# Two row tiles that take turns on PSUM banks: the turn signal moved from the SP queue to POOL, and one small product spread over a half tile

## The chip, the cores and the metric

The kernel runs on one core of a Trainium2 chip. The metric is the device time of one execution in microseconds (us), as the median of several runs.

In the views of the profile PE is TensorE's matmul, PEld its weight load, DVE VectorE, ACT ScalarE, POOL GpSimd and SP SyncE; a q behind a name stands for the instructions that its sequencer runs itself. A row of the windows view has the length of a stretch, then the busy time of PE, PEld, DVE, ACT and POOL (with the number of instructions), the granted clock, the busy share of the DMA engines and GB/s. All times are in us.

## The reference

A layer norm feeds a linear-attention block and a GEGLU feed-forward block, and both are added to the input. S = 2048 rows, D = 576, F = 4608, 32 heads of 18.

```python
xn = _layernorm(x, axis=-1)
return x + _A_ref(xn, A_wqkv, A_wo) + _B_ref(xn, B_w_gate, B_w_up, B_w_down)

# _B_ref: (gelu(x @ w_gate) * (x @ w_up)) @ w_down
# _A_ref: phi(q) @ (phi(k)^T v) / den, per head, then @ wo
```

## The kernel before

After the attention part (about 78 us) the kernel works through four groups of 512 rows. Each group has a gate/up stage of 18 blocks and a down stage of eight half tiles (128 rows by 288 columns of the output, each the sum of 36 down matmuls and five with `m_sb`). The sums stand in PSUM, in eight banks. A block has two units; a unit makes 128 gate and 128 up columns, on two 64-row tiles of the array that work at the same time. D = 576 is 4.5 x 128, so the halves of the fifth chunk of gate and up share one tile of weights (`wr`).

```python
class _Unit:
    def p1(self):                       # first phase: ten matmuls
        for kt in (4, 0, 1, 2, 3):
            self.mm(0, LO, kt, kt == 4, False)           # gate, upper 64 rows
            last = self.mm(1, HI, kt, kt == 4, False)    # up, lower 64 rows
        self.turn = nc.sync.nop()                        # the turn signal
        tc.add_manual_dep(self.turn.ins, last.ins.name, SYNC, ...)

    def p2(self):                       # second phase: eight matmuls, banks exchanged
        for kt in range(4):
            m = self.mm(1, LO, kt, False, kt == 3)
            if kt == 0:
                tc.add_manual_dep(m.ins, self.turn.ins.name, SYNC, ...)
            self.mm(0, HI, kt, False, kt == 3)
```

In the second phase each row tile writes the bank that the other one wrote before. The signal is an instruction without work: it waits until the last matmul of the first phase is done, and the first matmul of the second phase waits for it. It stands in the queue of SP, which issues all DMAs, behind the weight loads of the same unit:

```python
def gu_pair(sc, k):                     # one block
    ...
    for i in range(GUB):
        ...
        if blk > 0:
            load_gu(blk + NWBUF - 1, i) # two DMA issues on SP, for three blocks later
        u.p1()
        units.append((b, u))
    if sc == 0 and k >= 1:
        load_wd_slice()                 # one more DMA issue
    for i, (b, u) in enumerate(units):
        u.p2()
        ...                             # gelu on ACT, product on DVE

def den_norm(sc, c, q, pieces):         # ten of these in stage one, one after a block
    ...
    for h in range(0, w, P):
        nc.vector.reciprocal(out=d[:, h:h + P], in_=d[:, h:h + P])
    nc.gpsimd.tensor_tensor(out=pqT[:rows, c, cols], in0=pqT[:rows, c, cols], in1=d, op=ALU.mult)
```

The product kv x Wo (`m_stage`: ten matmuls of 288 columns into banks 2 to 7 in turn, each copied to `m_sb` by ACT) is made inside the first half tile of the first down stage, which needs it at its end:

```python
hooks = [{0: lambda: m_stage((0, 1, 2)), 16: lambda: m_stage((3, 4))} if sc == 0 else {}]
```

## Time and profile before

| | before |
|---|---|
| median of the first three runs | 532.59 us (532.07 to 533.6) |
| span of the profiled run | 530.5 us |
| TensorE busy | 99% |
| the four gate/up stages | 70.41, 71.39, 70.65, 70.50 us |
| first half tile, and an ordinary one | 7.35, 5.25 us |

### The profile page before, as it was taken

Reading aid. Unit: us, or ns where it says so; the run is one execution under the profiler, and the core shown is the slowest. Engines: PE = TensorE matmul, PEld = TensorE weight load, DVE = VectorE, ACT = ScalarE, POOL = GpSimd, SP = SyncE. Lnnn points to the kernel's source line nnn. Section 1 sums busy time; section 2 is a strip of 40 time slices with the busy share of each in tenths; the row PEclk is TensorE's granted clock in tenths of the full one; section 3 lists DMA queues with packets and bytes.
Section 4 is the critical chain, followed back from the end, with each engine's and each line's share of the span. In section 5 each row is a group of like instructions: output and inputs, shape, how many; then the busy total and the mean of one; then the engine's idle time right before and its main releaser. Section 6 shows DMA issues by size and latency. Waiting matters only on the chain.

```text
span 530.5 us, 10752 instructions
## 1 busy us (share of the span) xinstructions
PE 522.6 (99%) x4532; PEld 314.3 (59%) x4532; DVE 248.7 (47%) x408; ACT 152.5 (29%) x288; POOL 70.3 (13%) x83
## 2 busy tenths in 40 slices
PE   7999999999999999999999999999999999999997
PEld 5887666444467754444477744444677544445775
DVE  7885666783338613333368233333485143333101
ACT  6887783323330003323200022323100132322000
POOL 4666542110002100000012000000021000000000
PEclk9999999999999999999999999999999999999999
DMA  8910006898510025555400055555100345540000
GB/s 283 248 30 1 1 2 184 261 270 267 143 39 12 23 78 153 148 150 157 135 12 12 12 153 162 146 157 153 49 22 13 94 143 158 155 135 1 12 12 22
DMA packets 98810, 55.85 MB, mean 105 GB/s; under 512 B 5322, under 2 KB 98378, under 8 KB 98762
## 3 DMA queue, kind: packets, MB, share of 16 engines
q1 hardware_dynamic: 98762, 55.17, 36.2%
q8 instruction: 35, 0.57, 0.4%
q14 instruction: 13, 0.11, 0.1%
HBM read 52.79 MB, written 2.36 MB: 104 GB/s over the span
## 4 chain that ended last, share of the span: by engine, by line
PE 95%; SPq 2%; DVE 1%; ACT 1%; issue 0%; DMA 0%
PE ps_all L505 51%; PE ps_all L576 27%; PE ps_all L310 4%; PE ps_all L581 4%; PE ps_all L280 4%; PE ps_all L238 3%; PE ps_all L227 1%; SPq L166 1%; PE ps_all L370 1%; SPq L168 0%; SPq L169 0%; DMA x_sb<-in_A_x_dram 0%; ACT xnT L230 0%; DVE xn L217 0%; PE ps_all L358 0%
## 5 line engine op out<-in xcount | busy, mean ns | idle before, releaser
L505 PE MATMUL ps_all<-xnT,wg 64*128 64x512 bf16 x1152 | 274.1, 377 | 0.0
L505 PE MATMUL ps_all<-xnT,wu 64*128 64x512 bf16 x1152 | 272.6, 377 | 0.9 <-SPq L514 0.3
L549 DVE TENSOR_TENSOR hT<-ps_all,gl 128x512 bf16<-128x512 f32 x144 | 99.6, 692 | 168.9 <-ACT gl L548 168.7
L548 ACT ACTIVATE gl<-ps_all 128x512 f32<-128x512 f32 x144 | 86.0, 597 | 316.7 <-PE ps_all L505 294.9
L505 PEld LDWEIGHTS <-wu 64*128 64x128 bf16 x1152 | 106.9, 94 | 70.9 <-SPq L514 8.7
L505 PEld LDWEIGHTS <-wg 64*128 64x128 bf16 x1152 | 107.0, 94 | 66.7 <-issue 0.3
L576 PE MATMUL ps_all<-wd_sb,hT 128*128 128x288 bf16 x1152 | 146.6, 286 | 0.0
L576 PEld LDWEIGHTS <-hT 128*128 128x128 bf16 x1152 | 112.2, 98 | 31.5 <-issue 1.9
L384 DVE RECIPROCAL den_sb<-den_sb 126x128 f32<-126x128 f32 (+1 forms) x80 | 68.3, 911 | 0.5
L385 POOL TENSOR_TENSOR pqT<-pqT,den_sb 126x512 bf16<-126x512 bf16 (+3 forms) x25 | 24.1, 965 | 301.5 <-DVE den_sb L384 298.2
L584 DVE TENSOR_TENSOR res<-ps_all,x_sb 128x288 bf16<-128x288 f32 x32 | 14.6, 458 | 88.3 <-PE ps_all L581 88.3
L505 PE MATMUL ps_all<-xnT,wr 64*128 64x512 bf16 x288 | 55.9, 377 | 0.0
L581 PE MATMUL ps_all<-m_sb,pqT 126*128 126x288 bf16 (+1 forms) x160 | 24.9, 286 | 0.0
L505 PEld LDWEIGHTS <-wr 64*128 64x128 bf16 x288 | 14.6, 94 | 17.4 <-issue 1.1
L310 PE MATMUL ps_all<-xnT,wqkv_sb 128*126 128x512 bf16 (+1 forms) x100 | 24.4, 380 | 0.0
L265 POOL TENSOR_TENSOR hT<-phi_e,phi_a 128x576 bf16<-128x576 f32 x16 | 22.5, 1404 | 8.9 <-ACT phi_e L264 4.9
L280 PE MATMUL ps_all<-hT,xn 128*128 128x288 bf16 (+3 forms) x192 | 23.6, 266 | 0.0
L238 PE MATMUL ps_all<-wqkv_sb,xnT 128*128 128x288 bf16 x160 | 22.4, 286 | 0.8 <-DVE xnT L230 0.6
L280 PEld LDWEIGHTS <-xn 128*128 128x128 bf16 (+1 forms) x192 | 18.2, 101 | 4.5
L320 POOL TENSOR_TENSOR pqT<-phi_e,phi_a 126x512 bf16<-126x512 f32 (+1 forms) x14 | 17.7, 1268 | 15.5 <-DVE phi_a L318 11.8
L581 PEld LDWEIGHTS <-pqT 126*128 126x128 bf16 (+1 forms) x160 | 15.5, 97 | 4.1
L238 PEld LDWEIGHTS <-xnT 128*128 128x128 bf16 x160 | 15.0, 98 | 4.5 <-DVE xnT L230 0.8
(58 smaller groups left out, 200.6 us busy)
## 6 DMA issues: line engine op xcount, KB each, us to landing
wg<-in_B_w_gate_dram SPq DMA_DIRECT2D x72, 256.0 KB, 2.9
wu<-in_B_w_up_dram SPq DMA_DIRECT2D x72, 256.0 KB, 3.4
wd_sb<-in_B_w_down_dram SPq DMA_DIRECT2D x12, 432.0 KB, 4.5
wr<-in_B_w_gate_dram SPq DMA_DIRECT2D x72, 32.0 KB, 2.7
wr<-in_B_w_up_dram SPq DMA_DIRECT2D x72, 32.0 KB, 3.1
out_dram<-res SPq DMA_DIRECT2D x15, 144.0 KB, 1.8
x_sb<-in_A_x_dram SPq DMA_DIRECT2D x3, 576.0 KB, 6.6
wqkv_sb<-in_A_wqkv_dram SPq DMA_DIRECT2D x2, 576.0 KB, 9.2
```

The source lines that it names most:

```text
L238: nc.tensor.matmul(ps_all[:, k_bank(n, hf), :HALF], lhsT=xnT[:, kt, n * P:(n + 1) * P], rhs=wqkv_sb[:, kt, D + hf * HALF:D + (hf + 1) * HALF],
L265: nc.gpsimd.tensor_tensor(out=pk[:, n, :], in0=e[:], in1=a[:], op=ALU.add)
L280: nc.tensor.matmul(ps_all[:m, b, col:col + w], lhsT=xn[:, n, j0:j0 + m], rhs=pk[:, n, d0:d0 + w], start=(n == 0 and col == 0), stop=(n == ...
L310: nc.tensor.matmul(ps, lhsT=wqkv_sb[:, kt, q0:q0 + rows], rhs=xnT[:, kt, cs], start=(kt == 0), stop=(kt == KT - 1),)
L320: nc.gpsimd.tensor_tensor(out=pqT[:rows, c, cs], in0=e, in1=a, op=ALU.add)
L384: nc.vector.reciprocal(out=d[:, h:h + P], in_=d[:, h:h + P])
L385: nc.gpsimd.tensor_tensor(out=pqT[:rows, c, cols], in0=pqT[:rows, c, cols], in1=d, op=ALU.mult)
L505: return nc.tensor.matmul(self.outs[i], lhsT=self.lhs(i, rows, kt), rhs=self.rhs(i, rows, kt), start=start, stop=stop, skip_group_check=True,)
L548: nc.scalar.activation(out=gl[:], in_=ps_all[:, b[0], :], func=ACT.Gelu_apprx_tanh)
L549: nc.vector.tensor_tensor(out=hT[:, GUB * k + i, :], in0=ps_all[:, b[1], :], in1=gl[:], op=ALU.mult)
L576: nc.tensor.matmul(acc, lhsT=hT[:, f, j * P:(j + 1) * P], rhs=wd_sb[:, f, hs], start=(f == 0), stop=False,)
L581: nc.tensor.matmul(acc, lhsT=pqT[:rows, c, ts_], rhs=m_sb[:rows, c, hs], start=False, stop=(c == NCH - 1),)
```

## The change

The intent is to take the turn signal out of the queue in which DMA issues stand, and to end a wait in the first half tile. Three edits belong together. The signals go to POOL from the third block on. POOL's scaling product, which has to wait for reciprocals, is put one block later, behind the next block's signals. And the kv x Wo product is made two matmuls at a time, six down matmuls apart.

```diff
-        nc.gpsimd.tensor_tensor(out=pqT[:rows, c, cols], ..., in1=d, op=ALU.mult)
+        def scale():
+            nc.gpsimd.tensor_tensor(out=pqT[:rows, c, cols], ..., in1=d, op=ALU.mult)
+        return scale
...
-            self.turn = nc.sync.nop()
+            self.turn = self.relay.nop()
...
+            u = _Unit(..., nc.sync if blk < 2 else nc.gpsimd)
...
             gu_pair(sc, k)
+            if scales:
+                scales.pop(0)()
             if den_jobs:
-                den_norm(*den_jobs.pop(0))
+                scales.append(den_norm(*den_jobs.pop(0)))
...
-        hooks = [{0: lambda: m_stage((0, 1, 2)), 16: lambda: m_stage((3, 4))} if sc == 0 else {}]
+        hooks = [{6 * c_: (lambda c_=c_: m_stage((c_,))) for c_ in range(NCH)} if sc == 0 else {}]
```

More of the change, by code (lines that the diff above doesn't have):

```diff
@@ L384, in den_norm @@
             nc.vector.reciprocal(out=d[:, h:h + P], in_=d[:, h:h + P])
-        nc.gpsimd.tensor_tensor(out=pqT[:rows, c, cols], in0=pqT[:rows, c, cols], in1=d, op=ALU.mult)
+        def scale():
+            nc.gpsimd.tensor_tensor(out=pqT[:rows, c, cols], in0=pqT[:rows, c, cols], in1=d, op=ALU.mult)
+        return scale
     ln_stats(2)
@@ L473 @@
             kv_stage()
+    scales = []
     den_jobs = [(0, c, q, 2) for c in range(NCH) for q in range(2)]
@@ L498, with __init__ @@
     class _Unit:
-        def __init__(self, outs, lhs, rhs):
-            self.outs, self.lhs, self.rhs = outs, lhs, rhs
+        def __init__(self, outs, lhs, rhs, relay=nc.gpsimd):
+            self.outs, self.lhs, self.rhs, self.relay = outs, lhs, rhs, relay
         def mm(self, i, rows, kt, start, stop):
@@ L536, in lhs @@
                 return (wg, wu)[a][rows, kt, fcol]
-            u = _Unit([ps_all[:, b[0], :], ps_all[:, b[1], :]], lhs, lambda a, rows, kt: xnT[rows, kt, cs])
+            u = _Unit([ps_all[:, b[0], :], ps_all[:, b[1], :]], lhs, lambda a, rows, kt: xnT[rows, kt, cs],
+                      nc.sync if blk < 2 else nc.gpsimd)
             if blk > 0:
@@ L602, in dn @@
                     den_mm(nsc, c, banks.next())
-                    den_norm(nsc, c, 0, 1)
+                    den_norm(nsc, c, 0, 1)()
                 hooks.append({0: dn})
```

## The prediction

> **What bounds the kernel now.** I read the page's parts 1, 4 and 5 first, then the windows view cut at the stages, then the timeline at the places where the weight loads waited.
>
> The page says that TensorE never rests and that it is the chain that ended last:
>
> ```profile
> PE 522.6 (99%) x4532; PEld 314.3 (59%) x4532; DVE 248.7 (47%) x408; ACT 152.5 (29%) x288; POOL 70.3 (13%) x83
> PE 95%; SPq 2%; DVE 1%; ACT 1%; issue 0%; DMA 0%
> L505 PE MATMUL ps_all<-xnT,wg 64*128 64x512 bf16 x1152 | 274.1, 377 | 0.0
> L505 PE MATMUL ps_all<-xnT,wu 64*128 64x512 bf16 x1152 | 272.6, 377 | 0.9 <-SPq L514 0.3
> ```
>
> The reader is to see "SPq 2%" in the second line: L514 is the turn signal that the change moves, and the SP queue that carries it stands on the chain for some 10 us of 530. That is an upper limit and a misleading one: a piece of SP on the chain is a DMA issue that took some time, while TensorE was in most of that time still working on earlier matmuls. "PE 99%" misleads the other way: a matmul of 377 ns overlaps the next, so short pauses in issuing do not show as idle. I therefore measure the pauses by the pace of the stream. The windows view, cut at the first matmul of each gate/up stage and of each down stage, and once at the starts of twelve blocks in a row that show no wait, gives it:
>
> ```profile
> 97.40:144.03 46.63, 46.63 (x436) 20.97 (x433) 26.62 (x37) 14.33 (x24) 4.09 (x7) 1.00 0.82 240
> ...
> 77.59:148.00 70.41, 70.38 (x649) 34.05 (x648) 42.13 (x59) 23.64 (x39) 9.21 (x12) 1.00 0.75 219
> 148.00:191.51 43.51, 43.02 (x345) 33.77 (x343) 24.39 (x34) 3.69 (x11) 5.79 (x5) 1.00 0.04 12
> 191.51:262.90 71.39, 70.95 (x649) 30.92 (x649) 24.10 (x36) 20.91 (x35) 0.00 (x0) 1.00 0.53 151
> 262.90:304.33 41.43, 41.43 (x336) 32.53 (x335) 24.38 (x34) 0.60 (x1) 5.80 (x5) 1.00 0.04 14
> 304.33:374.98 70.65, 70.38 (x649) 31.22 (x649) 24.10 (x36) 20.91 (x35) 0.00 (x0) 1.00 0.54 153
> 416.40:486.90 70.50, 70.36 (x649) 31.15 (x648) 24.09 (x36) 20.90 (x35) 0.00 (x0) 1.00 0.45 129
> ```
>
> First column after the window: its length. Twelve blocks of 36 matmuls in 46.63 us are 3.886 us a block, the array's own pace at a clock of 1.00. A stage has 18 blocks, 69.95 us, and about 0.09 us more before the first down matmul, so 70.04 us without a pause. The four stages took 70.41, 71.39, 70.65 and 70.50: 0.37 + 1.35 + 0.61 + 0.46 = 2.79 us of pauses in all. That is everything that a better turn signal can win.
>
> Where the pauses are is in the timeline of the weight loads (bracket: idle before, and who ended it), beside the SP queue's rows:
>
> ```profile
> 92.63 0.09 PEld L505 LDWEIGHTS <-wu 64*128 64x128 bf16 x1 [0.53 <-SPq L514]
> 198.04 0.09 PEld L505 LDWEIGHTS <-wu 64*128 64x128 bf16 x1 [0.49 <-SPq L514]
> 199.23 0.09 PEld L505 LDWEIGHTS <-wu 64*128 64x128 bf16 x1 [0.65 <-SPq L514]
> ...
> 91.22 1.30 SPq L169 DMA_DIRECT2D wr<-in_B_w_up_dram  x1
> 196.34 1.59 SPq L166 DMA_DIRECT2D wr<-in_B_w_gate_dram  x1
> ```
>
> An issue of a wr load takes 0.51 us as a rule; now and then one takes 1.2 to 1.6 us. The turn signal stands behind it in the same queue, so the second phase of a unit starts late by what is over. The remaining cases are the first block of stages two to four, where the output store's wait for the last sum holds the same queue. A waiting load costs less than its bracket, since loads are spaced by some 0.12 us of idle anyway.
>
> **What the Trainium skill says.** "TensorEngine Tiling (Array Packing)", Restrictions and Gotchas: row tiles may not access one PSUM bank at the same time, and software has to synchronise them. So the signal cannot go; it can only be carried by someone else. The same page, Tiling Modes (Key Properties): a change of tiling mode drains TensorE. The trace agrees: five sums with m_sb take 0.62 us inside a down stage and 0.71 us before the switch to the 64-row tiles; both modes stay in the change, in the same number. "DMA: Bandwidth & Descriptors", Issuing engines are not separate DMA queues: spreading issues over engines saves only the sequencer's issue time. Here it is that time, 0.51 us and at times 1.59, that costs something, because a signal waits behind it. "Advanced Engine Details and Errata", Sequencer and Instruction Queues: engine instructions are pushed into a queue and wait there, control instructions run in the sequencer. So a signal on POOL should not have to wait for an elementwise product that is running; no row of the kernel before shows that for a signal.
>
> **The change part by part.**
>
> *The signal from SP to POOL.* 144 signals in 72 blocks; blocks 0 and 1 (4 signals) stay on SP, 140 move. No instruction is added; each stays a semaphore wait and a semaphore update, and in the built program POOL's signals get a semaphore of their own, not the one that its products count. PE's order is unchanged. What POOL has in front of a signal decides. In stages two to four it has nothing: its five products lie in the down stage, done four half tiles before the next signal (POOL 0.00 in those rows). So all pauses there should vanish: 1.35 + 0.61 + 0.46 = 2.42 us.
>
> *The deferred scaling.* In stage one POOL carries ten products of 0.67 us, each after two reciprocals on DVE:
>
> ```profile
> 86.97 1.75 DVE L384 RECIPROCAL den_sb<-den_sb 126x128 f32<-126x128 f32 x2
> ...
> 88.81 0.67 POOL L385 TENSOR_TENSOR pqT<-pqT,den_sb 126x256 bf16<-126x256 bf16 x1 [3.12 <-DVE den_sb L384]
> ```
>
> These reciprocals are those of block 1 (81.48 to 85.37); they end at 88.72, late in block 2. Left where it was, this product and its wait would stand before block 2's signals, due at about 85.37 + 1.28 = 86.65 us (the tenth matmul of a phase is issued 0.97 us after the first, and SP's signals in undisturbed blocks come some 0.3 us after that) and 87.7: late by some 1 to 2 us, ten times. Deferred by a block it stands after block 2's signals and before block 3's first, due at 89.25 + 1.28 = 90.5. The product ends at 89.48, so 1.0 us is left even if the signal had to wait for its end. Stage one should lose its pause too: 0.37 us. POOL answers 0.09 us after the reciprocal's end, which is quick enough: from the modelled end of a unit's last first-phase matmul to the weight load that needs the signal, there are 4 x 0.2155 - 0.377 = 0.48 us for the second unit of a block and more for the first.
>
> *The kv x Wo product over the first half tile.* Ten matmuls of 288 columns; before, six at the start and four after sixteen down matmuls. The windows for the first half tile and an ordinary one, and the timeline:
>
> ```profile
> 148.00:155.35 7.35, 6.87 (x54) 5.39 (x53) 1.28 (x3) 3.69 (x11) 0.00 (x0) 1.00 0.02 5
> 155.35:160.60 5.25, 5.25 (x43) 4.12 (x42) 4.45 (x7) 0.00 (x0) 0.64 (x1) 1.00 0.00 0
> ...
> 148.74 0.69 DVE L549 TENSOR_TENSOR hT<-ps_all,gl 128x512 bf16<-128x512 f32 x1 [0.17 <-ACT gl L548]
> 149.49 0.28 PE L559 MATMUL ps_all<-wo,kvT 126*126 126x288 bf16 x1 [0.44 <-DVE hT L549]
> ```
>
> The first costs 7.35 - 5.25 = 2.10 us more. The ten matmuls at the pace of the m_sb sums (0.62 / 5 = 0.124 us) are 1.24 us. The other 0.86 us is PE waiting: the fifth and sixth matmul want banks 6 and 7, which the last gelu and the last product of the stage are still reading until 149.43. In the change chunk 0 takes banks 2 and 3 (long free), chunk 1 comes at f = 6, about 148.0 + 0.25 + 6 x 0.1225 = 148.98, and wants bank 4 and 5, free at 148.57; chunk 2 comes at 149.96, after 149.43. Chunk 4 comes at f = 24, some 152.2, and is copied by ACT (0.32 us each) well before the sum reads it at about 153.7. So 0.86 us goes, all on the chain.
>
> Sum: 2.42 + 0.37 + 0.86 = 3.65 us. From the median 532.59 that is 528.9; from the profiled run, whose pauses I measured, 532.15 - 3.65 = 528.5. I take 528.7, 0.7% less.
>
> **The rivals.**
>
> *POOL is a slow messenger.* If every signal took over half a microsecond more than SP's, the 140 moved turns would each lose the excess: at 0.2 us each, 28 us slower. Against it stands the 0.09 us answer above.
>
> *POOL's products block the signals.* If the 1.0 us of room in stage one is not there, ten blocks lose up to 1 us each, and the time is 530 to 539. The 1.0 us is worked out from an unchanged DVE order, so I give this little.
>
> *The wait moves on.* SP, no longer held by the signals, may issue loads about 0.5 us earlier; the long issues of 1.2 to 1.6 us remain and only make loads late. They are used three blocks, 11.6 us, later and land in about 3 us, so nothing new should bind. If a pause remained anyway, the time would be near 531.
>
> *The spread product gains nothing.* Switching weights five times rather than twice could cost; but one den product inside a down stage costs 0.22 us for 512 columns, the mere pace. Without that gain the time is 529.6.
>
> **Range and chances.** The gain is capped at about 3.7 us by the pace of the array, so a gain over 2% (10.7 us) is out: 1%. Only the first two rivals make it slower by over 2%: 2%. The runs before spread by 1.5 us, probably with the number of long issues, which should matter less now. Range 527.6 to 530.4.
>
> **What would show it right or wrong.** Right: no weight load waiting for a signal, in blocks 2 and later; each of stages two to four at 70.0 to 70.1 us and stage one likewise; the first half tile near 6.5 us with no wait for hT; the long issues of SP still there, harmless. Wrong: weight loads waiting for POOL's signal in most blocks (slow messenger) or in stage one alone (products in the way), or waits for wg or wu landings.

## The result, and the profile after

The changed kernel took 528.99 us (median of six runs, 528.75 to 529.26), against 532.33 us for the kernel before (six runs, 531.39 to 533.6). The ratio is 0.9936, with a 95% interval of 0.9923 to 0.9949. The gain is 3.3 to 3.4 us, 0.6%.

First the chain that ended last, in the page of the changed kernel (shares of the span). The piece "SPq 2%" of before has gone:

```profile
PE 98%; DVE 1%; ACT 1%; DMA 0%; issue 0%
```

Then the windows view of the changed kernel, cut at the same places as before: stage one, the first down stage, and stages two to four. The first number after the window is its length.

```profile
77.75:147.95 70.20, 70.20 (x649) 44.64 (x649) 42.14 (x59) 23.65 (x39) 9.21 (x12) 1.00 0.75 219
147.95:190.66 42.71, 42.71 (x346) 33.79 (x345) 24.37 (x34) 3.98 (x11) 5.79 (x5) 1.00 0.04 12
190.66:260.70 70.04, 70.04 (x650) 31.46 (x649) 24.09 (x36) 20.91 (x35) 0.00 (x0) 1.00 0.54 155
302.12:372.16 70.04, 70.04 (x650) 31.46 (x649) 24.09 (x36) 20.91 (x35) 0.00 (x0) 1.00 0.54 154
413.57:483.61 70.04, 70.04 (x649) 31.46 (x649) 24.08 (x36) 20.91 (x35) 0.00 (x0) 1.00 0.46 130
```

Stages two to four take 70.04 us each, exactly the length worked out from the undisturbed pace. Between the two profiled runs the parts differ by -0.21 (stage one), -0.80 (first down stage), -1.35, -0.61 and -0.46 us (stages two to four), and by +0.16 us in the attention part. In sum that is -3.3 us; only the 0.16 us lies outside the places that the change touches. (The start of stage one lay between 77.59 and 78.02 us in all profiled runs, with no order to it.)

The groups view of the weight loads shows that nobody waits for the signal any more. First the kernel before, then the changed one (busy us, mean ns | idle before, who ended it):

```profile
L505 PEld LDWEIGHTS <-wu 64*128 64x128 bf16 x1152 | 106.9, 94 | 70.9 <-SPq L514 8.7
```

```profile
L509 PEld LDWEIGHTS <-wu 64*128 64x128 bf16 x1152 | 107.4, 94 | 61.8
```

And the timeline of the SP queue in the changed kernel shows that the long issues are still there:

```profile
91.38 1.21 SPq L169 DMA_DIRECT2D wr<-in_B_w_up_dram  x1
...
132.93 1.47 SPq L166 DMA_DIRECT2D wr<-in_B_w_gate_dram  x1
...
195.17 1.37 SPq L166 DMA_DIRECT2D wr<-in_B_w_gate_dram  x1
...
206.82 1.71 SPq L166 DMA_DIRECT2D wr<-in_B_w_gate_dram  x1
```

These take 1.2 to 1.7 us where 0.51 us is the rule; but no signal stands behind them, and what they load is needed three blocks later.

The trace's DMA packets say when such an issue comes. All 14 `wr` issues over 0.8 us in this run's gate/up stages, and all 13 in the kernel before, overlap a packet of kind "instruction" on queue 8 (16 KB, 0.9 to 1.8 us long), and each ends 0.40 to 0.43 us after that packet. Of the other 245 `wr` issues of the two runs three overlap one. So a long issue seems to wait for a fetch of instructions; no experiment here tested that.

The first half tile, again with an ordinary one below it:

```profile
147.95:154.49 6.54, 6.54 (x53) 5.36 (x53) 1.28 (x3) 3.98 (x11) 0.00 (x0) 1.00 0.04 8
154.49:159.74 5.25, 5.25 (x44) 4.13 (x42) 4.45 (x7) 0.00 (x0) 0.64 (x1) 1.00 0.00 0
```

It went from 7.35 to 6.54 us. The 1.29 us that it still takes over an ordinary one are the ten matmuls themselves.

### The profile page after: what moved, and what is told of

Same layout as the page of the kernel before. It is cut to its first block, busy times and chain, and to the rows that moved or that the text cites. A ratio compares the mean times of both kernels' runs of the same rounds, so it can differ in the third digit from the quotient of the medians.

```text
span 527.1 us, 10752 instructions
## 1 busy us (share of the span) xinstructions
PE 520.7 (99%) x4532; PEld 326.2 (62%) x4532; DVE 248.7 (47%) x408; ACT 152.8 (29%) x288; POOL 70.3 (13%) x83
## 4 chain that ended last, share of the span: by engine, by line
PE 98%; DVE 1%; ACT 1%; DMA 0%; issue 0%
PE ps_all L509 53%; PE ps_all L581 27%; PE ps_all L310 4%; PE ps_all L586 4%; PE ps_all L280 4%; PE ps_all L238 3%; PE ps_all L227 1%; PE ps_all L370 1%; DMA x_sb<-in_A_x_dram 0%; ACT xnT L230 0%; PE ps_all L564 0%; PE ps_all L358 0%; DVE xn L217 0%; DVE stats L206 0%; ACT rstd L213 0%; ACT rstd L214 0%
## 5 line engine op out<-in xcount | busy, mean ns | idle before, releaser
L509 PE MATMUL ps_all<-xnT,wu 64*128 64x512 bf16 x1152 | 268.4, 376 | 0.0
L509 PEld LDWEIGHTS <-wg 64*128 64x128 bf16 x1152 | 108.2, 94 | 62.6 <-issue 0.3
L509 PE MATMUL ps_all<-xnT,wr 64*128 64x512 bf16 x288 | 60.6, 376 | 0.0
L509 PEld LDWEIGHTS <-wr 64*128 64x128 bf16 x288 | 17.1, 94 | 16.3 <-issue 1.1
```

What stands on the lines that cost most here:

```text
L509: return nc.tensor.matmul(self.outs[i], lhsT=self.lhs(i, rows, kt), rhs=self.rhs(i, rows, kt), start=start, stop=stop, skip_group_check=True,)
```

## The experiments

The theory to test: there are two separate gains, one from taking the signal out of a queue in which it can be held up, and one from ending the wait for banks 6 and 7. Rivals: one of the parts gave all; POOL as such is a better or worse messenger; the deferral of the scaling product is needless; the room that the signal has is much smaller or larger than thought.

| run | median, us | before in the same rounds | ratio (95% interval) |
|---|---|---|---|
| signal alone | 529.76 | 532.42 | 0.9951 (0.9936 to 0.9965) |
| spread alone | 531.44 | 532.42 | 0.9977 (0.9961 to 0.9993) |
| no deferral | 539.61 | 532.42 | 1.0137 (1.0115 to 1.0158) |
| POOL from the start | 528.80 | 532.42 | 0.9932 (0.9917 to 0.9946) |
| SP, signals first | 529.06 | 532.73 | 0.9934 (0.9920 to 0.9947) |
| ACT as messenger | 528.83 | 532.73 | 0.9929 (0.9915 to 0.9942) |
| five hops | 528.85 | 532.73 | 0.9931 (0.9915 to 0.9947) |
| nine hops | 529.24 | 532.73 | 0.9937 (0.9921 to 0.9952) |
| thirteen hops | 530.70 | 532.63 | 0.9968 (0.9954 to 0.9983) |
| seventeen hops | 545.33 | 532.63 | 1.0242 (1.0225 to 1.0259) |

All ten gave correct results. The changed kernel was not run again in these rounds; its 528.99 us is from the first ones.

### The two parts one by one

Signal alone, from the changed kernel:

```diff
-        hooks = [{6 * c_: (lambda c_=c_: m_stage((c_,))) for c_ in range(NCH)} if sc == 0 else {}]
+        hooks = [{0: lambda: m_stage((0, 1, 2)), 16: lambda: m_stage((3, 4))} if sc == 0 else {}]
```

> The changed kernel with the kv x Wo product put back as six matmuls at the start and four after sixteen. Theory (two separate, additive gains): the gate/up stages stay at 70.04 us (70.20 in stage one), the first half tile is back at 7.1 to 7.35 us, so 2.5 to 2.7 us faster than before, about 529.8 against 532.3. Rival (the spread product gave it all): no gain, 532. Rival (the signal gave it all): 528.99 as the full change.

Spread alone, from the kernel before:

```diff
-        hooks = [{0: lambda: m_stage((0, 1, 2)), 16: lambda: m_stage((3, 4))} if sc == 0 else {}]
+        hooks = [{6 * c_: (lambda c_=c_: m_stage((c_,))) for c_ in range(NCH)} if sc == 0 else {}]
```

> The kernel before with the product spread, signals still on SP. Theory: the first half tile is 6.3 to 6.5 us and nothing else moves, so 0.8 us faster than before, about 531.5; weight loads still wait for the SP signal behind long DMA issues, about 15 to 20 times. Rival (the waits in the first half tile only move to where the sum reads m_sb): no gain.

The signal alone won 2.7 us and the spread alone 1.0 us (differences of medians; the kernel before spreads by over 2 us, so the last digit is not worth much). The profiles are sharper. The windows of the first half tile, first of the signal alone, then of the spread alone:

```profile
148.12:155.47 7.35, 6.87 (x54) 5.39 (x54) 1.28 (x3) 3.70 (x11) 0.00 (x0) 1.00 0.02 6
```

```profile
148.44:154.98 6.54, 6.54 (x54) 5.35 (x53) 1.29 (x3) 3.99 (x11) 0.00 (x0) 1.00 0.02 5
```

7.35 and 6.54 us are the lengths of the kernel before and of the changed one. With the signal alone, stages two to four took 70.04 us each; with the spread alone, they took 71.19, 70.35 and 70.63 us and 20 weight loads waited for SP. So the two gains are separate and add up.

### Is it SP, or the place in SP's queue?

Two kernels, both made from the kernel before with the product spread. In the first SP keeps the signals, but the loads are issued behind them:

```diff
-            if blk > 0:
-                load_gu(blk + NWBUF - 1, i)
             u.p1()
             units.append((b, u))
+        if blk > 0:
+            for i in range(GUB):
+                load_gu(blk + NWBUF - 1, i)
```

> Spread product, signals still on SP, but all four loads of a block issued behind both signals of that block. Normal issues (2.0 us) and one long one (1.1 us more) are over before the next block's first signal is due. Theory (it is the place in the queue and not the engine that counts): as fast as the changed kernel, 529.0 to 529.4, gate/up stages at 70.04 to 70.20 us. Rival (SP itself is the slower messenger, or loads that start 2 us later come late): 531 to 532, with weight loads waiting.

In the second ACT carries the signals, and the scaling products stay where they were:

```diff
-            self.turn = nc.sync.nop()
+            self.turn = nc.scalar.nop()
```

> Spread product, signals on ACT, scaling products not deferred. ACT's last gelu of a block starts 0.25 us into the next one and a signal is due at 1.4 us, so its sequencer is free. Theory: as fast as the changed kernel, 529.0, without its deferral. Rival (a signal waits for the running activate of 0.60 us, or gelu waits hold it): several us slower than 529.

Both are as fast as the changed kernel: 529.06 us (one of six runs took 529.71) and 528.83 us, stages two to four at 70.04 us. The windows of stage two, with SP and then with ACT:

```profile
190.56:260.60 70.04, 70.04 (x649) 31.46 (x649) 24.09 (x36) 20.91 (x35) 0.00 (x0) 1.00 0.51 147
```

```profile
190.69:260.73 70.04, 70.04 (x650) 31.46 (x649) 24.11 (x36) 20.93 (x35) 0.00 (x0) 1.00 0.54 155
```

With SP the groups view still has two short waits, which left no trace in the stage's length:

```profile
L505 PEld LDWEIGHTS <-wu 64*128 64x128 bf16 x1152 | 107.8, 94 | 65.1 <-SPq L514 0.6
```

So it is not the engine that mattered. It was what stood in front of the signal: all three queues did whose earlier work was over when the signal was due, even SP's own in another order, without deferral and without a second engine. With ACT the program needs two edits (the signal's engine and the spread product) in place of three.

### Is the deferral needed, and what does a signal pass?

```diff
-                scales.append(den_norm(*den_jobs.pop(0)))
+                den_norm(*den_jobs.pop(0))()
```

> The changed kernel with each scaling product issued at once, in front of the next block's signals. A scaling product whose wait stands in POOL's sequencer (jobs 2, 4, 6, 8: two semaphores) holds back the first signal of the next block until the reciprocals end, about 1.44 us too late. Theory A (a signal passes a product that waits in the engine's own queue, jobs 1, 3, 5, 7, 9 with one semaphore): four pauses, 5.8 us, about 534.5. Theory B (a signal also waits for the start of a queued product): nine pauses, 13 us, about 542. Theory C (for its end): nine pauses of 2.1 us, about 548. Rival (deferral is needless): 529.

The time was 539.61 us, 10.6 us more than the changed kernel. The windows of its stage one, and of the nine blocks with a pause:

```profile
77.69:158.72 81.03, 71.76 (x649) 32.49 (x649) 42.14 (x59) 23.65 (x39) 9.21 (x12) 1.00 0.66 190
85.47:131.43 45.96, 36.69 (x327) 15.50 (x325) 27.50 (x37) 10.86 (x19) 6.35 (x10) 1.00 0.73 210
```

45.96 / 9 = 5.11 us a block where 3.886 is the pace: nine pauses of 1.22 us. So theory B holds, and A and C fall. The timeline of the first pause, from three engines:

```profile
87.07 1.75 DVE L384 RECIPROCAL den_sb<-den_sb 126x128 f32<-126x128 f32 x2
```

```profile
88.91 0.67 POOL L387 TENSOR_TENSOR pqT<-pqT,den_sb 126x256 bf16<-126x256 bf16 x1 [3.12 <-DVE den_sb L384]
```

```profile
88.94 0.09 PEld L509 LDWEIGHTS <-wu 64*128 64x128 bf16 x1 [1.48 <-POOLq L518]
```

The reciprocals end at 88.82. Only then does the signal behind the product come, at 88.87 in the trace's records, with the product's own row starting at 88.91; the signal's matmuls were done nearly two microseconds before. This product had one semaphore to wait for, in its own instruction, as in five of the nine pauses; in all five the signal came 0.04 us before the product's row. So on POOL a signal does not pass a product that waits for a semaphore. (In the other four pauses the wait stood in POOL's sequencer, in front of the signal; theory A had counted these as pauses too.) The next signal came at 88.97, while the product ran from 88.91 to 89.58. A signal does pass a product that runs.

The pause was 1.22 us rather than the 1.44 that I expected. The weight load came late by what was said; but the matmul then followed its load at once, while in the undisturbed stream it follows one slot (0.21 us) later. That raised the question of how much room the signal really has; see the last four runs.

### Does POOL have to be spared in the first two blocks?

```diff
-                      nc.sync if blk < 2 else nc.gpsimd)
+                      nc.gpsimd)
```

> The changed kernel with the signals of blocks 0 and 1 on POOL too. POOL's sequencer takes up its last wait for the attention part at 79.59 us, and the first signal is needed by 79.66. Theory (a signal passes running products): no loss or under 0.1 us, 529.0. Rival (it waits for the two products that run until 81.6 us): the first block is 2 us longer, about 531.

528.80 us, stage one at 70.20 us as in the changed kernel, no load waiting for a signal. The exception for the first two blocks isn't needed. It is another case of a signal that passes running products.

### How late may the messenger be?

The signal was passed on several times between POOL and ACT:

```diff
-            self.turn = self.relay.nop()
-            tc.add_manual_dep(self.turn.ins, last.ins.name, SYNC, ...)
+            hops = 5 if self.relay is nc.gpsimd else 1          # 9, 13, 17
+            for hop in range(hops):
+                self.turn = (self.relay if hop % 2 == 0 else nc.scalar).nop()
+                tc.add_manual_dep(self.turn.ins, last.ins.name, SYNC, ...)
+                last = self.turn
```

> The changed kernel with every moved signal passed on four times more between POOL and ACT before TensorE sees it (five hops), to make the messenger late on purpose. In the changed kernel the signal of the second unit comes 0.43 us before its weight load and the shortest such distance seen was 0.04 us, so the spare is some 0.38 us. Theory: as long as the four hops take under 0.38 us together, no loss, 529.0; if more, 70 times the excess.

> The same with nine hops. Theory: the loss per block is eight hops' time less 0.38 us, 70 times; at some 0.06 us a hop that is 0.10 us a block, 7 us, about 536; at 0.08 us a hop 18 us, about 547. Rival (signals have far more room than the weight load's place tells, because only the matmul needs them): no loss.

A hop took 0.048 us (four in 0.192 us, eight in 0.383 us by the semaphore records). Five hops cost nothing and nine cost 0.3 us in all. My lower estimate for nine had been 7 us, with 0.06 us a hop; at 0.048 us nine hops use up just the 0.38 us that I had read as spare, so this run could not tell whether the spare ends there. Two more did:

> The changed kernel with thirteen hops. A hop was measured at 0.048 us, so the signal is 12 x 0.048 = 0.58 us later: 0.42 + 0.58 = 0.99 us after the last first-phase matmul, and the weight load at 1.04 us instead of 0.86. Theory L (a late weight load is a loss): 0.18 us a block, 70 blocks, 12.6 us, about 541.5. Theory M (only the matmul has to start in time, at 1.076 us; with nine hops and without deferral it followed its load by anything from 0.21 down to 0.00 us): no loss or a few us at most, 529 to 531.

> The same with seventeen hops: 16 x 0.048 = 0.77 us later, signal at 1.19 us and load at 1.23 us. Theory L: 0.37 us a block, 26 us, about 555. Theory M: the matmul starts at 1.24 us instead of 1.076, 0.16 us a block, 11 us, about 540.

The groups view of thirteen hops, then of seventeen:

```profile
L509 PEld LDWEIGHTS <-wu 64*128 64x128 bf16 x1152 | 102.5, 94 | 75.0 <-POOLq L520 26.8
```

```profile
L509 PEld LDWEIGHTS <-wu 64*128 64x128 bf16 x1152 | 98.9, 94 | 94.0 <-POOLq L520 59.4
```

With thirteen hops 81 loads waited, 26.8 us in sum, and the time rose by only 1.7 us. Theory L (a late load is a loss) falls: it wanted 12.6 us. Even the 1.7 us is not the price of the usual delay: in the trace nearly all of it lies in 13 blocks in which a hop took 0.31 to 0.35 us instead of 0.048, and the other 55 that could be measured lost 0.14 us together. With seventeen hops all 140 waited and the time rose by 16.3 us. Theory M had 11: in most blocks the loss was 0.19 to 0.20 us, close to the 0.16 worked out, and the rest comes from blocks in which the hops together took up to 1.07 us instead of 0.77, again through one slow hop. Why a hop is slow at times was not tested. It was not ACT's gelus: no ACT operation ran during any of the 17 slow hops. A hint is that 16 of the 17 were followed within 2 us by an 8 KB packet of kind "instruction" on queue 14, of which the trace has 30 in 544 us. So the second unit's signal, which comes 0.42 us after the start of the last first-phase matmul, may come about 0.6 us later before it costs anything.

## Why the prediction was right

Predicted were 528.7 us (527.6 to 530.4), and 528.99 was measured. The steps, one by one:

- *Most of the 2% on the chain is no loss, and the pace of the stream tells what is.* Right. Read from the chain, the gain would have been some 10 us; read from the pace, 2.79 us at most. The stages won 2.63 us.
- *Stages two to four, 2.42 us.* Right to 0.01 us: they lost 1.35, 0.61 and 0.46 us and stand at 70.04 us.
- *Stage one, 0.37 us.* Too much: it won 0.21 us and stands at 70.20, not 70.04 us. The term that was mis-sized is the floor of this stage. In its first block the second unit's up matmul waits for a bank that DVE reads until 78.97 us, and from there the row tile with the lower rows runs behind the other by 0.17 us. Both then keep their pace, so the distance stays, and at the switch to the full array the later one counts. The timeline of the last matmuls of the stage in the changed kernel, then in the one without deferral, where the pauses had brought the tiles together again:

```profile
147.47 0.38 PE L509 MATMUL ps_all<-xnT,wu 64*128 64x512 bf16 x1
147.65 0.38 PE L509 MATMUL ps_all<-xnT,wg 64*128 64x512 bf16 x1
147.95 0.46 PE L564 MATMUL ps_all<-wo,kvT 126*126 126x288 bf16 x2
```

```profile
158.41 0.38 PE L509 MATMUL ps_all<-xnT,wu 64*128 64x512 bf16 x1
158.41 0.38 PE L509 MATMUL ps_all<-xnT,wg 64*128 64x512 bf16 x1
158.72 0.46 PE L564 MATMUL ps_all<-wo,kvT 126*126 126x288 bf16 x2
```

  The pause of 0.37 us in the kernel before had done the same, so 0.16 us of it was not to be won.
- *Products in the way without deferral: late by some 1 to 2 us, ten times.* Right in kind and size: nine times 1.22 us, the tenth product standing before a block whose signals stay on SP.
- *A signal is due 1.28 us after its block's start.* Right as a sum, by luck, since two errors cancel: in the trace of the kernel before, the tenth matmul is issued 0.87 us after the first, not 0.97, and the signal comes 0.41 us later, not 0.3. Two smaller misreadings changed nothing either: a pair of matmuls takes 3.886 / 18 = 0.216 us, not 0.2155, and POOL's last product of a down stage is done some 11 us before the next signal, which is two half tiles and not four.
- *POOL answers fast enough.* Right. Signals came a median 0.42 us after the start of the last first-phase matmul on POOL and 0.41 us on SP. The rival of the slow messenger had its threshold at half a microsecond; the hops put it at about 0.6 us. It had the cost too high: 140 turns were to lose, but seventeen hops took 0.19 us from most blocks, once a block, because the first unit of a block has more room.
- *The spread product, 0.86 us.* Right: 0.81 us in the half tile, and the same in the run that had this part alone.
- *The wait moves on.* It did not. No wait for a load that landed late took the place of the old one, with the long issues still there.

The profiled run won 3.31 us of the 3.65. Stage one fell short by 0.16 us and the half tile by 0.05, and the attention part, which the change does not touch, came out 0.16 us longer.

## What to carry to other kernels

A signal that is needed within a microsecond should not stand in a queue behind anything that takes a variable time to issue, or that itself waits for a semaphore; check what is in front of it first, since reordering the same queue may do as well as another engine. Measure pauses of a pipelined engine by its pace against an undisturbed stretch, not by its busy share or by the share of a releaser on the chain. And when several small matmuls need banks that are just being read out, place them where the banks are already free.

## What the Trainium skill lacked or had wrong

- "Advanced Engine Details and Errata", Sequencer and Instruction Queues, has engine instructions wait for semaphores in a queue of their own, and leaves open what a signal behind such an instruction does. On POOL it came only when the product's semaphore had come (88.87 after reciprocals that ended at 88.82), in five cases of five; behind a product that ran it came at once (88.97, with the product running until 89.58).
- "DMA: Bandwidth & Descriptors", Issuing engines are not separate DMA queues, calls the issue time usually small relative to the DMA. It lacks that the time varies: 0.51 us as a rule for a `wr` load, and up to 1.7 us now and then, which holds up whatever stands behind. It lacks too what the long ones go with: 27 of 27 overlapped a 16 KB packet of kind "instruction".
- "TensorEngine Tiling (Array Packing)" says that tiles operate independently, and lacks that two row tiles fed by one stream stay apart by what one of them once waited (0.17 us here) until a wait for both, and that this is paid at the next mode switch (stage one 70.20 us, the others 70.04 us).
